# Pooled attention's products taken by turns over the array's column groups, and the last 64 tokens' products and transposes on whole 128-row blocks

## The chip, the cores and the metric

The kernel runs on one core of one Trainium2 chip. The metric is device time in microseconds, the median of repeated executions. The kernel before takes 795.58 us (median of 3, 794.69 to 795.67). TensorE (PE) multiplies, VectorE (DVE), ScalarE (ACT) and GpSimd (POOL) do the elementwise work, SyncE (SP) and ACT issue DMAs.

## The reference

Three stages follow each other: attention (a pooled one plus a local one), a token and channel mixer, and a mixer with sine and cosine.

```python
B, H, S, D = 4, 8, 576, 64; factor = 4; scale = 1 / sqrt(D)
# pooled attention: means over 4 tokens, 144 queries and keys a head
q_d, k_d, v_d = (t.reshape(B, H, S // 4, 4, D).mean(axis=3) for t in (q, k, v))
out_up = repeat(softmax(scale * q_d @ k_d.T) @ v_d, 4, axis=2)
# local attention: |i - j| < 4
out_local = softmax(where(mask, scale * q @ k.T, -1e9)) @ v
x = (out_up + out_local).transpose(0, 2, 1, 3).reshape(B, S, H * D)
# mixer 1: over tokens (576 -> 256 -> 576), then over channels (512 -> 1536 -> 512)
h = relu(x.transpose(0, 2, 1) @ w_tok1) @ w_tok2
u = x + h.transpose(0, 2, 1)
x = u + relu(u @ w_ch1) @ w_ch2
# mixer 2
theta = x @ w_theta
y = w_tok_r @ (x * cos(theta)) + w_tok_i @ (x * sin(theta))
u = x + y
out = u + relu(u @ w_ch)
```

All mixer weights arrive as 64-bit floats.

## The kernel before

The weights are read as pairs of 32-bit words and turned into a high and a low 32-bit part (`weights`, L109 to L153: two ACT passes, a clamp on POOL or DVE, four passes on DVE, one copy on ACT, a subtraction on POOL, a sum on DVE or POOL). Each mixer product is the sum of three (`mm3`, L100): high by high, high by low, low by high. The attention products are plain 32-bit ones; the trace records each of those as two passes, so that 32 products have 64 records.

There are three stretches. First comes the attention stage, up to the end of `ORDER`: for every batch and half of the heads it runs a pooled attention (`quad_front`, events F), four local ones (`pair_local`, L) and the token mixer (`token_mix`, T), mixed with the weight conversions and with channel mixing of the first half of the channels for batches 0 and 1 (C0, C1). The list `ORDER` (L28) says in which order the pieces are emitted; a list scheduler then places each engine's instructions by priority and its own estimate of time, so that an edit in one place moves instructions on every engine. Second, the attention stage's memory is released, and the second half of the channel weights and the weights of mixer 2 are loaded through ACT's DMA queue (`rawq`, L114, L635) and converted beside channel mixing. Third is mixer 2.

In `quad_front` the scores `sd` (L338) and their exponents `pd` are transposed on PE (`pdt`, L383) into `pts`. The second product `od` (L393 to L400) has 144 query rows: its outputs stand in four groups `c` of 32 PSUM partitions, which are the array's four groups of 32 columns. For each group in turn: one product with 260 moving columns (L393), four with 65 (L396), one with 65 in a region of its own (L399), one more added there (L400). All have 128 rows of stationary data and 32 columns. `sd` (L338, L347), the local scores `s` (L448) and the local products `o` (L485) have 64 rows or fewer by 32 columns, and walk over row and column groups by turns.

The tokens 512 to 575 are half a block of 128. In `token_mix` block 4 of the input has the tokens in its first 64 rows; rows 64 to 127 hold copies for the product `xs` (L539), which joins two 64-row products with the low parts. L538 multiplies 64 rows alone; L564 transposes 64 rows to 64 columns. In `pair_local` L476 transposes the ninth slot of `pbuf` (128 rows by 64 columns).

Of the kernel before, what the change touches and what calls it, by code (L numbers as in the profile page):

```python
# [11 lines left out]
F32 = mybir.dt.float32  # L12
# [27 lines left out]
DTOK = 256  # L40
DCH = 1536
NB = 5

NS = 9

STEP, HEADROOM = 102, 2
W = 38
# [4 lines left out]
HEAD = [0, 2, 1, 3]  # L52
# [9 lines left out]
def kernel(  # L62
# [20 lines left out]
    act, dve, pool, pe = nc.scalar, nc.vector, nc.gpsimd, nc.tensor  # L83
# [7 lines left out]
    idt = const.tile([128, 128], F32, name="idt")  # L91
# [144 lines left out]
    with ExitStack() as actx:  # L236
        sb1 = actx.enter_context(tc.tile_pool(name="a1", bufs=1))
# [19 lines left out]
        zero = sb1.tile([128, 384], BF16, name="zero")  # L257
# [6 lines left out]

        msk = sb1.tile([128, NB, W], F32, name="msk")

        pbuf = [sb1.tile([128, NS, 64], F32, name=f"pbuf{i}") for i in range(2)]
        for t in pbuf:
            pool.memset(t, 0.0)

        w1h = sb1.tile([128, 5, DTOK], F32R, name="w1h")
# [6 lines left out]
        def load_tok1():  # L278
            for kb in range(4):
                weights(stg, w1h[:, kb, :], w1l[:, kb, :], [(0, 128, w_tok1[kb * 128 : (kb + 1) * 128, :])])  # L280
            last = w_tok1[512:576, :]
            weights(stg, w1h[:, 4, :], w1l[:, 4, :], [(0, 64, last), (64, 128, last)])
            act.copy(w1s[0:64, :], w1h[0:64, 4, :].bitcast(F32))
            act.copy(w1s[64:128, :], w1l[64:128, 4, :].bitcast(F32))

        def load_tok2():
            for kb in range(2):
# [18 lines left out]
        def quad_front(b, hh):  # L306
# [6 lines left out]
            for p in range(2):  # L313
                p4 = 2 * hh + p
                q, k = loaded[b, p4]
                for src, dst in ((q, qd), (k[:, 3 : 3 + S], kd)):
                    src = src.rearrange("p (s r) -> p s r", r=4)
                    h = sb1.tile([128, SD, 2], F32, tag="qa", name=f"qa_{at}", bufs=1)
# [69 lines left out]
            act.copy(pts[:, 4:7].rearrange("p a n -> p (a n)"), pt[:, 1, 0:384])  # L388
            yield
            od = mmp.tile([128, 512], F32, tag="mm", name=f"od_{at}")  # L390
            for c in range(4):
                r = slice(32 * c, 32 * c + 32)
                pe.matmul(od[r, 0:260], pts[:, 5, r], vl.rearrange("p h d -> p (h d)"), start=True, stop=False)  # L393
                for i in range(4):
                    h = HEAD[i]
                    pe.matmul(  # L396
                        od[r, 65 * h : 65 * h + 65], pts[:, i, r], vs[:, h, :], start=False, stop=(i == 3)
                    )
                pe.matmul(od[r, 260:325], pts[:, 6, r], vl[:, HEAD[c], :], start=True, stop=False)  # L399
                pe.matmul(od[r, 260:325], pts[:, 4, r], vs[:, HEAD[c], :], start=False, stop=True)  # L400
            odv = od[:, 0:325].rearrange("p (h n) -> p h n", h=5)
            rd = sb2.tile([128, 5, 1], F32, tag="rd", name=f"rd_{at}")
# [38 lines left out]
        def pair_local(b, p4):  # L441
            hh, p = divmod(p4, 2)
            at = f"{b}_{p4}"
            q, k = loaded[b, p4]
            s = wide("s", f"s_{at}")
            warm(s[:, 0, 192:512], (12 if b == 0 else 0) + (12 if b == p4 == 0 else 0))
            for i, j, r, g in groups:
                pe.matmul(  # L448
                    s[r : r + 32, j, i // 2 * W : i // 2 * W + W],
                    q[64 * j : 64 * j + 64, 32 * g : 32 * g + 32],  # L450
                    k[64 * j : 64 * j + 64, 32 * g : 32 * g + W],
                    start=True,
                    stop=True,
                )
            pb = pbuf[p4 % 2]
            pv = pb[:, :, 0:W]
            dve.tensor_tensor(
                out=pv[:, 0:8].rearrange("p (b j) n -> p j b n", j=2),
                in0=s[:, :, 0 : 4 * W].rearrange("p j (b n) -> p j b n", n=W),
                in1=msk[:, 0:4].unsqueeze(1).to_broadcast([128, 2, 4, W]),  # L460
                op=ALU.add,
            )
            for j in range(2):
                r = slice(64 * j, 64 * j + 64)
                dve.tensor_tensor(out=pv[r, 8], in0=s[r, j, 4 * W : 5 * W], in1=msk[r, 4], op=ALU.add)
            mx = sb2.tile([128, NS, 1], F32, tag="mx", name=f"mx_{at}")
            dve.tensor_reduce(out=mx, in_=pv, axis=AX.X, op=ALU.max)
            dve.tensor_tensor(out=pv, in0=pv, in1=mx.to_broadcast([128, NS, W]), op=ALU.subtract)
            exps[b, p4] = act.activation(pv, pv, AF.Exp, scale=1.0 / math.sqrt(D))
            yield  # L470
            pt = wide("big", f"pt_{at}")
            pts = sb2.tile([128, NB, 128], F32, tag="plt", name=f"plt_{at}")
            warm(pt[:, 1, 128:512], 12 if b == 0 else 0)
            for blk in range(4):
                pe.transpose(pt[:, 0, blk * 128 : (blk + 1) * 128], pb[:, 2 * blk : 2 * blk + 2, :].rearrange("p j n -> p (j n)"), idt)
            pe.transpose(pt[0:64, 1, 0:128], pb[:, 8, :], idt)  # L476
            act.copy(pts[:, 0:4].rearrange("p b n -> p (b n)"), pt[:, 0, :])
            act.copy(pts[0:64, 4], pt[0:64, 1, 0:128])
            yield
            vw = values[b, p4]  # L480
            o = blocks(wide("o", f"o_{at}"), 65)
            for i, j, r, g in groups:

                h = 0 if i == 8 else 64 * j
                pe.matmul(  # L485
                    o[r : r + 32, 4 if i == 8 else 5 * j + i // 2],
                    pts[h : h + W, i // 2, r : r + 32],
                    vw[h : h + W, g + 2 * j if i == 8 else g, :],
                    start=True,
                    stop=True,  # L490
                )
            rl = sb2.tile([128, 2 * NB, 1], F32, tag="rl", name=f"rl_{at}")
            dve.tensor_scalar(out=rl[:, 0:NS], in0=o[:, 0:NS, 64:65], scalar1=1e-9, scalar2=None, op0=ALU.add)
            dve.reciprocal(out=rl[:, 0:NS], in_=rl[:, 0:NS])
            x = x_of(b, hh)
            dve.tensor_tensor(  # L496
                out=x[:, p, 0:4].rearrange("p b (j n) -> p j b n", j=2),
                in0=o.rearrange("p (j b) n -> p j b n", j=2)[:, :, 0:4, 0:64],
                in1=rl.rearrange("p (j b) n -> p j b n", j=2)[:, :, 0:4].to_broadcast([128, 2, 4, 64]),
                op=ALU.mult,  # L500
            )
            dve.tensor_tensor(
                out=x[:, p, 4, 0:64], in0=o[:, 4, 0:64], in1=rl[:, 4].to_broadcast([128, 64]), op=ALU.mult
            )
            yield
            xu, xe = xus[b, hh]
            xv = x[:, p, 0:4]
            uv = xu[:, 0:4, p * 128 : (p + 1) * 128]
            pool.tensor_tensor(out=xv, in0=xv, in1=uv, op=ALU.add)  # L509
            xv = x[:, p, 4, 0:64]  # L510
            pool.tensor_tensor(out=xv, in0=xv, in1=xe[:, p * 64 : (p + 1) * 64], op=ALU.add)
            halves[b, hh] = halves.get((b, hh), 0) + 1
            if halves[b, hh] == 2:

                first, second = x[:, :, 4, 0:64], x[:, :, 4, 64:128]
                act.copy(second[0:64], first[64:128])
                act.copy(second[64:128], first[64:128])
                act.copy(first[64:128], first[0:64])
            yield

        def token_mix(b, hh):
# [11 lines left out]
            for tb in range(2):  # L533
                ps = mmp.tile([128, 512], F32, tag="mm", name=f"t1_{at}_{tb}")
                t = slice(tb * 128, (tb + 1) * 128)
                for kb in range(4):
                    mm3(ps[:, 0:DTOK], w1h[:, kb, t], w1l[:, kb, t], xh[:, :, kb], xl[:, :, kb], kb == 0, False)
                pe.matmul(ps[:, 0:DTOK], w1h[0:64, 4, t], xh[0:64, :, 4], start=False, stop=False)  # L538
                pe.matmul(ps[:, 0:DTOK], w1s[:, t], xs, start=False, stop=True)  # L539
                h1 = sb2.tile([128, DTOK], F32R, tag="h1", name=f"h1_{at}_{tb}")  # L540
                h2 = sb2.tile([128, DTOK], F32R, tag="h2", name=f"h2_{at}_{tb}")
                act.activation(h1, ps[:, 0:DTOK], AF.Relu)
                dve.scalar_tensor_tensor(
                    out=h2, in0=ps[:, 0:DTOK], scalar=0.0, in1=h1.bitcast(F32), op0=ALU.max, op1=ALU.subtract
                )
                hs.append((h1, h2))
                yield
# [4 lines left out]
            for db in range(2):  # L552
# [3 lines left out]
                for th, (t0, t1) in enumerate(((0, cut), (cut, S))):  # L556
# [2 lines left out]
                    xt = mmp.tile([128, 512], F32, tag="mm", name=f"xt_{at}_{db}_{th}")  # L559
                    first = t0 // 128  # L560
                    for blk in range(first, (t1 + 127) // 128):
                        m = 128 if blk < 4 else 64
                        o = (blk - first) * 128
                        pe.transpose(xt[:, o : o + m], x[0:m, db, blk], idt[0:m, 0:m])  # L564
                    o = t0 - first * 128
                    act.copy(u, xt[:, o : o + n])
                    ps = mmp.tile([128, 512], F32, tag="mm", name=f"t2_{at}_{db}_{th}")
# [296 lines left out]
```

## Time and profile before

| | us |
|---|---|
| median of 3 runs | 795.58 (794.69 to 795.67) |
| the profiled execution | 796.43, its span 794.6 |
| PE busy | 748.0 (94%) |
| DVE busy | 508.9 (64%) |
| ACT, POOL busy | 334.6, 269.5 |
| chain of waits, shares | PE 60%, DVE 21%, DMA 7%, issue 5%, POOL 3% |

The span is cut into 40 equal slices of 19.9 us here; each digit is an engine's busy share in tenths. The last row is the granted TensorE clock in tenths.

```
PE   7788897899999999999889889999999999999998
DVE  5999988863555333379999999722395266455432
PEclk9888998799999999999999999999999999999999
```

PE is busy nearly all the time outside slices 0 to 7 and 19 to 24, and in those two regions DVE is. The share of busy time alone does not say what an engine waits for; the stretches are read apart in the rows below.

### The profile page before, as it was taken

To read this page: it belongs to the slowest core of one execution; us is meant where nothing else is said; L and a number is where in the kernel's file an instruction comes from. 1 tells how busy PE (TensorE), PEld (TensorE's weight loads), DVE (VectorE), ACT (ScalarE), POOL (GpSimd) and SP (SyncE) were. 2 spreads that over 40 slices of the span, in tenths; PEclk is the share of its full clock that TensorE was granted. 3 is DMA by queue.
4 is the path that set the end of the run, shared out by engine and by line. 5 is a ranking of instruction groups with operands and counts; after the bars stand their busy time and mean duration, and the time that the engine had idled before them with its cause. 6 is when DMAs were issued, how large, how long until landed. Compare 5 with 4: busy or idle time off the path is not lost.

```text
span 794.6 us, 19303 instructions
## 1 busy us (share of the span) xinstructions
PE 748.0 (94%) x7872; PEld 697.6 (88%) x7872; DVE 508.9 (64%) x1151; ACT 334.6 (42%) x773; POOL 269.5 (34%) x292
## 2 busy tenths in 40 slices
PE   7788897999999999999889889999999999999998
PEld 4566676888988999999889889999999999999998
DVE  5999988863555333379999999722395266455432
ACT  2555745533334223155556555421285064253210
POOL 1667677732021010078879889300000000000000
PEclk9888998799999999999999999999999999999999
DMA  9578366355423202144646764531000210300101
GB/s 285 161 233 235 115 191 183 93 149 154 154 85 93 85 30 91 60 150 153 193 156 192 239 205 144 162 111 61 31 2 1 90 38 1 120 1 1 61 1 60
DMA packets 61897, 90.73 MB, mean 114 GB/s; under 512 B 10096, under 2 KB 39920, under 8 KB 61808
## 3 DMA queue, kind: packets, MB, share of 16 engines
q1 hardware_dynamic: 53456, 73.70, 30.4%
q10 hardware_dynamic: 8352, 15.80, 6.3%
q8 instruction: 62, 1.02, 0.5%
q14 instruction: 27, 0.22, 0.1%
HBM read 69.42 MB, written 20.05 MB: 113 GB/s over the span
## 4 chain that ended last, share of the span: by engine, by line
PE 60%; DVE 21%; DMA 7%; issue 5%; POOL 3%; ACT 2%; SPq 2%; DVEq 0%; ACTq 0%; POOLq 0%
PE y L103 5%; PE y L101 5%; PE y L102 5%; DVE ww L137 4%; PE c L226 4%; PE c L229 4%; PE c L227 4%; PE c L101 3%; PE c L102 3%; PE c L103 3%; DVE ww L129 2%; DVE we L140 2%; DVE wf L147 2%; POOL ww L125 2%; PE th L101 2%
## 5 line engine op out<-in xcount | busy, mean ns | idle before, releaser
L125 POOL TENSOR_SCALAR ww<-ww 128x256 f32<-128x256 f32 (+1 forms) x85 | 101.2, 1197 | 51.7 <-ACT ww L124 49.9
L103 PE MATMUL y<-wrh,zl 128*128 128x288 f32 x256 | 75.7, 296 | 0.0
L102 PE MATMUL y<-wrl,zh 128*128 128x288 f32 x256 | 75.6, 295 | 0.0
L101 PE MATMUL y<-wrh,zh 128*128 128x288 f32 x256 | 75.6, 296 | 0.0
L218 DVE SCALAR_TENSOR_TENSOR g<-c,g 128x288 fp32r<-128x288 f32 x96 | 43.2, 452 | 48.0 <-ACT g L217 47.6
L226 PE MATMUL c<-g,c21h 128*128 128x288 f32 x192 | 54.4, 305 | 11.1 <-ACT g L217 11.0
L217 ACT ACTIVATE g<-c 128x288 fp32r<-128x288 f32 x96 | 38.7, 408 | 58.1 <-PE c L103 58.0
L101 PE MATMUL c<-uh,c10h 128*128 128x288 f32 x192 | 58.4, 309 | 0.7 <-DVE g L218 0.7
L103 PE MATMUL c<-uh,c10l 128*128 128x288 f32 x192 | 57.8, 302 | 0.0
L102 PE MATMUL c<-ul,c10h 128*128 128x288 f32 x192 | 57.1, 298 | 0.0
L226 PE MATMUL c<-g,c20h 128*128 128x288 f32 x192 | 54.6, 309 | 2.5 <-ACT g L217 2.0
L101 PE MATMUL c<-uh,c11h 128*128 128x288 f32 x192 | 56.9, 296 | 0.0
L122 ACT ACTIVATE wf<-raw 128x256 bf16<-128x256 uint32 (+1 forms) x91 | 40.3, 443 | 39.2 <-DVE wrl L150 6.0
L102 PE MATMUL c<-ul,c11h 128*128 128x288 f32 x192 | 56.7, 295 | 0.0
L509 POOL TENSOR_TENSOR x<-x,xu 128x512 f32<-128x512 f32 x16 | 23.1, 1454 | 98.7 <-DVE x L496 51.8
L103 PE MATMUL c<-uh,c11l 128*128 128x288 f32 x192 | 56.5, 294 | 0.0
L227 PE MATMUL c<-g,c21l 128*128 128x288 f32 x192 | 53.4, 301 | 0.0
L227 PE MATMUL c<-g,c20l 128*128 128x288 f32 x192 | 53.4, 300 | 0.0
L129 DVE TENSOR_SCALAR ww<-ww 128x256 uint32<-128x256 uint32 (+1 forms) x91 | 46.3, 510 | 5.2 <-POOL ww L125 5.0
L231 DVE TENSOR_TENSOR ut<-c,ut 128x288 f32<-128x288 f32 x56 | 25.3, 451 | 36.7 <-PE c L229 36.5
L226 PEld LDWEIGHTS c<-g,c21h 128*128 128x128 f32 x192 | 36.9, 192 | 13.5 <-ACT g L217 13.5
L137 DVE SCALAR_TENSOR_TENSOR ww<-raw,ww 128x256 uint32<-128x256 uint32 (+1 forms) x91 | 47.8, 528 | 1.1
(202 smaller groups left out, 2394.1 us busy)
## 6 DMA issues: line engine op xcount, KB each, us to landing
raw<-w_ch ACTq DMA_DIRECT2D x32, 256.0 KB, 2.9
ut<-uT SPq DMA_DIRECT2D x14, 576.0 KB, 4.3
xT<-ut SPq DMA_DIRECT2D x14, 576.0 KB, 3.1
raw<-w_ch SPq DMA_DIRECT2D x24, 256.0 KB, 3.4
vd<-vtok SPq DMA_DIRECT2D x8, 650.0 KB, 6.0
raw<-w_ri ACTq DMA_DIRECT2D x18, 288.0 KB, 3.0
k<-kT SPq DMA_DIRECT2D x16, 291.0 KB, 5.1
q<-qT SPq DMA_DIRECT2D x16, 288.0 KB, 3.8
```

What stands on the lines that cost most here:

```text
L101: pe.matmul(out, lh, rh, start=start, stop=False)
L102: pe.matmul(out, lh, rl, start=False, stop=False)
L103: pe.matmul(out, ll, rh, start=False, stop=stop)
L122: act.activation(f, words[:, :, 0], AF.Copy, scale=2.0**-52)
L125: next(clamps).tensor_scalar(out=w, in0=w, scalar1=F64_LEAST, scalar2=F64_MOST, op0=ALU.max, op1=ALU.min)
L129: dve.tensor_scalar(out=wu, in0=wu, scalar1=3, scalar2=0x3FFFFFF8, op0=ALU.logical_shift_left, op1=ALU.bitwise_and,)
L137: dve.scalar_tensor_tensor(out=wu, in0=words[:, :, 1], scalar=0xC0000000, in1=wu, op0=ALU.bitwise_and, op1=ALU.bitwise_or)
L217: act.activation(h1, ps[:, 0:HALF], AF.Relu)
L218: dve.scalar_tensor_tensor(out=h2, in0=ps[:, 0:HALF], scalar=0.0, in1=h1.bitcast(F32), op0=ALU.max, op1=ALU.subtract)
L226: pe.matmul(ps[:, 0:HALF], w2h[:, cb, d], hs[cb][0], start=(cb == 0), stop=False)
L227: pe.matmul(ps[:, 0:HALF], w2l[:, cb, d], hs[cb][0], start=False, stop=False)
L229: pe.matmul(ps[:, 0:HALF], w2h[:, cb, d], hs[cb][1], start=False, stop=(cb == NCB - 1))
```

## The change

The `od` products are emitted by rounds: the four 260-column products, one for each column group, then the four groups' products for each head, then the four L399s, then the four L400s. The products themselves and their number stay. The ninth slot of `pbuf` gets a tenth, always zero, beside it, so that its transpose is a 128 by 128 one. L538 takes all 128 rows: rows 64 to 127 of the weight block are set to zero once by a copy on ACT, after the two copies that need them. The transposes of block 4 in `token_mix` take all 128 rows and columns.

```diff
-        pbuf = [sb1.tile([128, NS, 64], F32, name=f"pbuf{i}") for i in range(2)]
+        pbuf = [sb1.tile([128, NS + 1, 64], F32, name=f"pbuf{i}") for i in range(2)]
...
             act.copy(w1s[64:128, :], w1l[64:128, 4, :].bitcast(F32))
+
+            act.copy(w1h[64:128, 4, :], zero[64:128, 0:DTOK])
...
-            for c in range(4):
-                r = slice(32 * c, 32 * c + 32)
+
+            rows = [slice(32 * c, 32 * c + 32) for c in range(4)]
+            for r in rows:
                 pe.matmul(od[r, 0:260], pts[:, 5, r], vl.rearrange("p h d -> p (h d)"), start=True, stop=False)
-                for i in range(4):
-                    h = HEAD[i]
-                    pe.matmul(
-                        od[r, 65 * h : 65 * h + 65], pts[:, i, r], vs[:, h, :], start=False, stop=(i == 3)
-                    )
+            for i in range(4):
+                h = HEAD[i]
+                for r in rows:
+                    pe.matmul(od[r, 65 * h : 65 * h + 65], pts[:, i, r], vs[:, h, :], start=False, stop=(i == 3))
+            for c, r in enumerate(rows):
                 pe.matmul(od[r, 260:325], pts[:, 6, r], vl[:, HEAD[c], :], start=True, stop=False)
+            for c, r in enumerate(rows):
                 pe.matmul(od[r, 260:325], pts[:, 4, r], vs[:, HEAD[c], :], start=False, stop=True)
...
-            pv = pb[:, :, 0:W]
+            pv = pb[:, 0:NS, 0:W]
...
-            for blk in range(4):
-                pe.transpose(pt[:, 0, blk * 128 : (blk + 1) * 128], pb[:, 2 * blk : 2 * blk + 2, :].rearrange("p j n -> p (j n)"), idt)
-            pe.transpose(pt[0:64, 1, 0:128], pb[:, 8, :], idt)
+            for blk in range(NB):
+                src = pb[:, 2 * blk : 2 * blk + 2, :].rearrange("p j n -> p (j n)")
+                pe.transpose(pt[:, blk // 4, blk % 4 * 128 : blk % 4 * 128 + 128], src, idt)
...
-                pe.matmul(ps[:, 0:DTOK], w1h[0:64, 4, t], xh[0:64, :, 4], start=False, stop=False)
+                pe.matmul(ps[:, 0:DTOK], w1h[:, 4, t], xh[:, :, 4], start=False, stop=False)
...
-                        m = 128 if blk < 4 else 64
                         o = (blk - first) * 128
-                        pe.transpose(xt[:, o : o + m], x[0:m, db, blk], idt[0:m, 0:m])
+                        pe.transpose(xt[:, o : o + 128], x[:, db, blk], idt)
```

PE, the `od` of batch 1's second half of the heads, before (`c` is channel mixing; the pattern of four rows stands four times):

```order
L101 MATMUL c_0_0_1_3_3217<-uh_0_1_3156,c10h 128x288
L393 MATMUL od_1_2861<-vl_1_2571,pts_1_2805 32x260
L396 MATMUL od_1_2861<-vs_1_2569,pts_1_2805 32x65 x4
L399 MATMUL od_1_2861<-vl_1_2571,pts_1_2805 32x65
L400 MATMUL od_1_2861<-vs_1_2569,pts_1_2805 32x65
L393 MATMUL od_1_2861<-vl_1_2571,pts_1_2805 32x260
...
```

The same place in the changed kernel (L396, L400, L402 and L404 are its new line numbers):

```order
L489 MATMUL o_1_2910<-vw_1_2534,plt_1_2854 32x65 x14
L396 MATMUL od_1_2862<-vl_1_2572,pts_1_2806 32x260 x4
L400 MATMUL od_1_2862<-vs_1_2570,pts_1_2806 32x65 x16
L402 MATMUL od_1_2862<-vl_1_2572,pts_1_2806 32x65 x4
L404 MATMUL od_1_2862<-vs_1_2570,pts_1_2806 32x65 x4
L489 MATMUL o_1_2910<-vw_1_2534,plt_1_2854 32x65 x13
```

The group's products now follow each other by kind, and it stands between local products `o` where it stood within channel mixing.

PE, the last transposes of the token mixer (`xt`, batch 3), before:

```order
L229 MATMUL c_2_0_0_3_5111<-g_2_0_0_5_5048,c20h 128x288
L564 MATMUL xt_1_1_1_4911<-idt,x_1_4692 128x128 x2
L564 MATMUL xt_1_1_1_4911<-idt,x_1_4692 128x64
L101 MATMUL c_2_0_1_0_5228<-uh_0_1_5224,c10h 128x288
L102 MATMUL c_2_0_1_0_5228<-ul_0_1_5225,c10h 128x288
```

The same in the changed kernel:

```order
L226 MATMUL c_2_0_0_3_5112<-g_2_0_0_2_4997,c20h 128x288
L567 MATMUL xt_1_1_1_4912<-idt,x_1_4693 128x128 x3
L227 MATMUL c_2_0_0_3_5112<-g_2_0_0_2_4997,c20l 128x288
L226 MATMUL c_2_0_0_3_5112<-g_2_0_0_3_5014,c20h 128x288
```

The 64-column transpose is a third whole one, and the group moved forward past the end of a channel product: 727 channel products stand ahead of the attention stage's last instruction on PE before, 715 now.

ACT, the end of the attention stage, where it issues the first load of the second weights (`raw`), before (`us` is the token mixer's result, `g` a channel product's):

```order
L566 COPY us_1_1_4898<-xt_1_1_1_4911 128x320
L217 ACTIVATE g_2_0_1_0_5241<-c_2_0_1_0_5228 128x288
L217 ACTIVATE g_2_0_1_1_5258<-c_2_0_1_1_5245 128x288
L114 DMA raw<-w_ch 128x256 x2
L217 ACTIVATE g_2_0_1_2_5275<-c_2_0_1_2_5262 128x288
```

The same in the changed kernel:

```order
L569 COPY us_1_1_4899<-xt_1_1_1_4912 128x320
L217 ACTIVATE g_2_0_1_0_5242<-c_2_0_1_0_5229 128x288
L114 DMA raw<-w_ch 128x256 x3
L217 ACTIVATE g_2_0_1_1_5259<-c_2_0_1_1_5246 128x288
```

The loads stand one channel block earlier in ACT's queue.

## Rows read from the trace of the kernel before

**Rows 1.** Busy time by stretch: us, then each engine, granted clock, DMA share, GB/s.

```profile
20.00:160.00 140.00, 119.15 (x1999) 95.31 (x1997) 128.05 (x324) 78.79 (x215) 99.97 (x111) 0.85 0.59 174
160.00:337.00 177.00, 175.13 (x2326) 159.15 (x2325) 79.60 (x198) 55.02 (x130) 24.19 (x29) 1.00 0.33 99
337.00:505.00 168.00, 153.11 (x1106) 148.62 (x1105) 153.71 (x342) 91.26 (x227) 140.88 (x144) 0.99 0.58 181
```

**Rows 2.** Timeline of ACT where the attention stage ends: start, length, instruction.

```profile
336.17 0.41 ACT L217 ACTIVATE g<-c 128x288 fp32r<-128x288 f32 x1 [1.17 <-PE c L103]
336.72 0.91 ACTq L114 DMA_DIRECT2D raw<-w_ch  x2
337.75 0.41 ACT L217 ACTIVATE g<-c 128x288 fp32r<-128x288 f32 x1 [1.17 <-PE c L103]
```

**Rows 3.** Timeline of PE over one `od` group, the eighth.

```profile
257.76 0.62 PE L393 MATMUL od<-vl,pts 128*32 128x260 f32 x2
258.22 0.62 PE L396 MATMUL od<-vs,pts 128*32 128x65 f32 x8
258.68 0.22 PE L399 MATMUL od<-vl,pts 128*32 128x65 f32 x1
258.68 0.41 PE L393 MATMUL od<-vl,pts 128*32 128x260 f32 x1
...
258.79 0.28 PE L400 MATMUL od<-vs,pts 128*32 128x65 f32 x2
...
261.56 0.28 PE L400 MATMUL od<-vs,pts 128*32 128x65 f32 x2
261.77 0.26 PE L448 MATMUL s<-k,q 64*32 64x38 f32 x4
```

**Rows 4.** Timeline of PE's weight loads in the same group.

```profile
258.68 0.14 PEld L393 LDWEIGHTS od<-vl,pts 128*32 128x32 f32 x2
```

**Rows 5.** Groups of PE's instructions up to 330 us, forms apart.

```profile
L393 PE MATMUL od<-vl,pts 128*32 128x260 f32 x64 | 20.5, 402 | 0.0
...
L538 PE MATMUL t<-xh,w1h 64*128 64x256 f32 x16 | 6.9, 431 | 0.0
...
L564 PE MATMUL xt<-idt,x 64*128 64x64 f32 x15 | 4.1, 273 | 0.0
```

**Rows 6.** Timeline of PE, one group of local products.

```profile
120.13 1.09 PE L485 MATMUL o<-vw,plt 38*32 38x65 f32 x72
```

**Rows 7.** Timeline of PE without the 64-row product L538 (87 us), and with it.

```profile
87.28 0.28 PE L102 MATMUL t<-xl,w1h 128*128 128x256 f32 x1
...
87.63 0.28 PE L101 MATMUL t<-xh,w1h 128*128 128x256 f32 x1
...
241.41 0.28 PE L102 MATMUL t<-xl,w1h 128*128 128x256 f32 x1
...
242.28 0.28 PE L102 MATMUL t<-xl,w1h 128*128 128x256 f32 x1
```

**Rows 8.** Timeline of PE: three transposes, the last of 64 rows (294 us); whole ones.

```profile
294.24 0.58 PE L564 MATMUL xt<-idt,x 128*128 128x128 f32 x3
...
295.00 0.31 PE L102 MATMUL t<-w2l,h 128*128 128x320 f32 x1
...
300.51 0.38 PE L475 MATMUL pt<-idt,pbuf 128*128 128x128 f32 x2
...
300.83 0.38 PE L564 MATMUL xt<-idt,x 128*128 128x128 f32 x2
...
301.19 0.29 PE L102 MATMUL c<-ul,c10h 128*128 128x288 f32 x1
```

**Rows 9.** The chain of waits, 84 to 112 us: start, length, what.

```profile
105.31 1.01 PE od L393 x2
```

**Rows 10.** Timeline of PE at a wait.

```profile
127.41 1.09 PE L475 MATMUL pt<-idt,pbuf 128*128 128x128 f32 x4 [3.24 <-DVE x L502]
```

**Rows 11.** Busy time after that wait, columns as in rows 1.

```profile
128.00:132.00 4.00, 3.59 (x16) 3.21 (x15) 3.86 (x13) 2.70 (x9) 2.81 (x5) 0.50 1.02 222
```

## The prediction

> **What bounds the kernel now.** I read the busy time by stretch first, because the share over the whole span (PE 94%) mixes stretches with different limits. From 160 to 337 us PE is busy 175.13 of 177.00 us at the full granted clock, DVE only 79.60: here a microsecond of PE is a microsecond of the kernel. From 20 to 160 us DVE is busy 128.05 of 140 us and PE 119.15 at a mean clock of 0.85: here the weight conversions bind, and PE counts only where the chain runs through it. From 337 to 505 us DVE is at 153.71 and POOL at 140.88 of 168 us, and PE has 15 us idle [rows 1]. After 505 us PE is full again, as the last slices of the page show; the change touches nothing there.
>
> The second view is ACT's queue at the border. The loads that feed the bound of 337 to 505 us are issued at 336.72, after the attention stage has let go of its memory [rows 2]. So that stretch hangs on the end of the attention stage and moves forward with it as a block; what PE saves ahead of it is not eaten by PE's idle time in it.
>
> The third view is PE's timeline of one `od` group. Its first pass starts at 257.76 and the next product after it at 261.77: 4.01 us. A 260-column product (two passes) holds its column group for 0.46 us, from 257.76 to 258.22; four 65-column products (eight passes) for another 0.46, so 0.057 a pass. Only at the border of two column groups do two of them work at once: at 258.68 the next group's 260-column pass starts in the same moment as this group's first L399, and this group's L400 still follows at 258.79, two passes of 0.055 later, as fast as without a neighbour [rows 3]. So column groups do run side by side, and the order of the program is what keeps three of the four idle. The weight load of that neighbour also starts at 258.68, under the running product [rows 4].
>
> **The change part by part.** *The `od` rounds.* Each column group has 0.46 + 12 x 0.057 = 1.15 us of work (two long passes, eight of L396, four of L399 and L400). If the four groups run beside each other, that is the time of the whole `od`. What lies behind its last pass stays: that pass starts 0.06 after 261.56, and the next product 0.15 later, at 261.77, so about 0.1 more than a pass. The new step is 1.26 us; saved 2.75 a group. That more than two tiles run at once is shown by the local products, which go round eight tiles: 72 passes in 1.09 us, 0.22 of it the last one's length, so 0.012 a pass against 0.057 here [rows 6]. The bounds: at best the 64 passes at 0.012, which the 1.15 us of one group's own work forbids; at worst no gain, 4.01. I take 1.26, next to the rows of the local products. There are eight groups (64 records of L393, eight each [rows 5]); four of them start after 160 us, the one of rows 3 last: 4 x 2.75 = 11.0 us.
>
> The weighing of a rule. The row shows a load into one column group while another column group's product runs, both on all 128 rows [rows 4]. The Trainium skill says otherwise: in "TensorE: Matmul & The Clock Gate", Part 3, a weight load overlaps a running product only when their row groups differ. All `od` products use the same four row groups, so by that rule each load would wait for the product ahead and the rounds would gain nothing. The trace speaks against it at this place, and the rule stands below as a rival.
>
> *The 64-row product (L538).* With it, four steps from one L102 to the next take 242.28 - 241.41 = 0.87 us; three plain steps take 87.63 - 87.28 = 0.35, so four 0.47 [rows 7]. The excess is 0.40 us, and it is not the product itself (256 columns either way) but the two changes between 64-row and 128-row tiling, each with a wait on both sides. Of the 16 [rows 5] ten lie after 160 us: 4.0 us.
>
> *The 64-row transposes (L564).* Three transposes and the first product behind them take 295.00 - 294.24 = 0.76 us. With whole ones it is 301.19 - 300.83 = 0.36 for two and the product, and 0.107 more for a third ((300.83 - 300.51) / 3): 0.47 [rows 8]. Saved 0.29. Of the 16 (one is past the row's 330 us) eleven lie in the PE-bound stretch; six stand before 128-row work and save 0.29, five before 64-row products, where one of the two changes stays, and I give these 0.1, a third. Together 2.2 us.
>
> *The transposes of the ninth slot (L476)* take 0.10 us, 300.73 to 300.83, as long as the whole one beside them: nothing. *The zero copy* on ACT is one more of the two 64 by 256 copies there, 0.40 us in a queue that is busy 78.79 of 140 us [rows 1]; DVE's conversions cover it, and uncovered it costs 0.4 once. *The larger memset* of `pbuf` is 11% of 0.58 us, twice, before the first load lands: nothing, at most 0.13.
>
> *What the scheduler moved.* On PE the changes between 64-row and 128-row forms, counted in the order from the fifth `od` on, go from 94 to 69. The edits alone take away 32 (two for each of ten L538s and six L564s), so seven came back, at about 0.17 each: 1.2 us lost. ACT issues the second weights' loads one channel block earlier, and a block is 337.75 - 336.17 = 1.58 us [rows 2]: 1.6 gained. The work jumped over lands in the next stretch, where PE has 15 us to spare.
>
> *Before 160 us* there are four `od` groups, six L538s and five L564s, some 15 us of PE. DVE's 91% bounds what can come of it: between 0 and 10. Only one of the groups is on the chain, at 105.31, with its first product at half speed in either order (1.01 instead of 0.46 us) [rows 9]: 2.75 saved there as well. With 0.4 for each of three L538s I take 4; behind it DVE's queue is late next.
>
> *The sum.* 11.0 + 4.0 + 2.2 - 1.2 + 1.6 + 4 = 21.6 us. From the profiled execution's own 796.43 that leaves 774.8; the median of the runs shown is 0.85 below it, so I predict 774.
>
> **The rivals.** *One pass at a time per group.* The first pass of each product runs beside the others' work, but its second pass holds up the issue behind it. Then a group costs one pass of every product: 16 x 0.057 + 8 x 0.057 + 4 x 0.23 = 2.3 us, 2.4 with the tail, and the saving falls to 1.6: 4.6 us less in the bound stretch, about 1 less before it, 780. For it: inside one column group passes are strictly serial [rows 3]. Against it: 0.012 a pass in the local products, each of which is a pair too [rows 6].
>
> *No overlap: the change doesn't do what it says.* The `od` stays at 4.01; left are 4.0 + 2.2 - 1.2 + 1.6 and 1 before 160 us: 788. Against it: rows 3 and 4. This is what the skill's rule on row groups gives.
>
> *The end of the attention stage is set by something other than PE.* A faster PE then waits for DVE, POOL or the trip of `od` through memory. In the bound stretch PE idles only 1.9 us [rows 1], so nothing shows yet, but little shows how far behind the next chain is. If half of the 17 us there is lost: 783 to 785.
>
> *More comes before 160 us.* All of DVE's idle time goes, 10 instead of 4: 768.
>
> *Slower: the clock.* At 127.41 PE had waited 3.24 us for DVE, and the granted clock in the next four microseconds was 0.50 [rows 10, 11], that is 1.2 GHz instead of 2.4. The two slices of 19.9 us from there on have 8 and 7 tenths of the clock on the page, so up to 0.5 x 19.9 = 10 us were lost to it. PE now reaches DVE's results sooner, so such waits can appear between 160 and 337 us, where there is none now. Each costs up to 3 + 10 us; two use up the gain, and from there on the kernel is slower: 796 to 800.
>
> **How the numbers follow.** Forecast 0.60 (own range 769 to 780), one pass at a time 0.13, no overlap 0.06, another end 0.08, more before 160 us 0.06, the clock 0.07. The range for 8 in 10 is 765 to 787, from the case with more to the edge of no overlap. A measurement of this kernel can tell about 0.2%, 1.6 us. Only the clock reaches that on the other side; I split it 0.04 slower and 0.03 the same. Faster is 0.93.
>
> **What would show it.** In the new trace the first passes of the four long `od` products start within a few hundredths of a microsecond and a whole `od` lasts about 1.2 us; 2.4 is the first rival, 3.9 the second. The 64-row product's steps become 0.12 us. The first `raw` load of ACT is issued between 312 and 318 us, and from there to the end of the conversions it is again some 168 us. The prediction fails if PE has idle time or a clock below 1.00 in the stretch before that load, or if the conversions afterwards take longer than before.

## The result, and the profile after

The changed kernel takes 771.94 us (median of 4, 770.8 to 773.74) against 795.13 for the kernel before beside it: a ratio of 0.9714, 95% interval 0.9688 to 0.9741. The forecast was 774 with a range of 765 to 787. A second measurement on another chip gave 773.15 against 795.8, 0.9721 (0.9702 to 0.974). The profiled execution has a span of 768.9 us, 25.7 less than before, and lies at the lower end of the four. In the table of the experiments one execution of 2314.4 us (C1 last, again) was in a slower state and is left out of its median.

First the same view as [rows 1], cut where the parts of the program end: at the first load of the second weights, at the end of their conversion, at the end. Before the change (us, PE, weight loads, DVE, ACT, POOL, granted clock, DMA share, GB/s):

```profile
0.00:336.72 336.72, 308.71 (x4566) 263.30 (x4567) 217.75 (x548) 138.72 (x354) 127.73 (x147) 0.93 0.47 141
336.72:507.10 170.38, 155.49 (x1124) 151.00 (x1123) 155.72 (x347) 91.66 (x228) 141.73 (x145) 0.99 0.58 181
507.10:794.60 287.50, 283.77 (x2186) 283.33 (x2185) 135.40 (x258) 104.19 (x191) 0.00 (x0) 1.00 0.13 43
```

And after:

```profile
0.00:314.18 314.18, 273.35 (x4554) 236.53 (x4555) 219.99 (x547) 136.86 (x354) 126.18 (x147) 0.94 0.51 150
314.18:480.00 165.82, 156.15 (x1125) 151.35 (x1124) 153.78 (x347) 92.37 (x229) 139.24 (x145) 0.99 0.60 185
480.00:768.90 288.90, 285.14 (x2197) 284.71 (x2195) 135.82 (x259) 104.33 (x191) 0.00 (x0) 1.00 0.14 44
```

Ahead of the first load PE has 35.4 us less to do, and 12.8 us of that became idle time (28.0 before, 40.8 now); 22.5 us are gained there. The conversions are 4.6 us shorter and what follows 1.4 longer: 3.2 more. The counts of PE differ by 12, the channel products that moved across the border.

The `od` group that answers to [rows 3], timeline of PE:

```profile
239.73 0.65 PE L396 MATMUL od<-vl,pts 128*32 128x260 f32 x8
240.19 0.64 PE L400 MATMUL od<-vs,pts 128*32 128x65 f32 x32
240.65 0.29 PE L402 MATMUL od<-vl,pts 128*32 128x65 f32 x8
240.76 0.30 PE L404 MATMUL od<-vs,pts 128*32 128x65 f32 x8
240.99 0.37 PE L452 MATMUL s<-k,q 64*32 64x38 f32 x32
```

From 239.73 to 240.99 are 1.26 us, where it was 4.01. Eight long passes take 0.46, as two did; 32 short ones take 0.46, as eight did: four column groups at once, each at the pace that it has alone. The weight loads of the eight long passes, from PE's timeline of loads, start together with them, while the passes take until 240.19:

```profile
239.73 0.16 PEld L396 LDWEIGHTS od<-vl,pts 128*32 128x32 f32 x8
```

The place of [rows 7]: L542 is the product that had 64 rows.

```profile
225.36 0.28 PE L102 MATMUL t<-xl,w1h 128*128 128x256 f32 x1
225.48 0.28 PE L103 MATMUL t<-xh,w1l 128*128 128x256 f32 x1
225.60 0.28 PE L542 MATMUL t<-xh,w1h 128*128 128x256 f32 x1
225.72 0.29 PE L102 MATMUL t<-xl,w1h 128*128 128x256 f32 x1
```

It has become one step of 0.12 among others. Its weight load starts at 225.48, in the moment in which the product L103 ahead of it starts on the same 128 rows and 128 columns:

```profile
225.48 0.19 PEld L542 LDWEIGHTS t<-xh,w1h 128*128 128x128 f32 x1
```

The transposes, answering to [rows 8]:

```profile
298.94 0.49 PE L567 MATMUL xt<-idt,x 128*128 128x128 f32 x3
299.19 0.38 PE L226 MATMUL c<-g,c20h 128*128 128x288 f32 x1
299.40 0.30 PE L227 MATMUL c<-g,c20l 128*128 128x288 f32 x1
```

Three transposes and the product behind them take 0.46 us, 0.76 before. ACT's queue at the border, answering to [rows 2]:

```profile
313.63 0.41 ACT L217 ACTIVATE g<-c 128x288 fp32r<-128x288 f32 x1 [3.78 <-PE c L103]
314.18 1.38 ACTq L114 DMA_DIRECT2D raw<-w_ch  x3
```

The first load is issued at 314.18, inside the 312 to 318 that the prediction named, behind one channel block's `g` instead of two.

### The profile page after: what moved, and what is told of

The parts are those of the page before. It is cut to its first block, busy times and chain, and to the rows that moved or that the text cites. A ratio compares the mean times of both kernels' runs of the same rounds, so it can differ in the third digit from the quotient of the medians.

```text
span 768.9 us, 19289 instructions
## 1 busy us (share of the span) xinstructions
PE 714.6 (93%) x7872; PEld 672.6 (87%) x7872; DVE 509.6 (66%) x1151; ACT 333.6 (43%) x774; POOL 265.4 (35%) x292
## 4 chain that ended last, share of the span: by engine, by line
PE 60%; DVE 23%; DMA 6%; issue 6%; POOL 2%; SPq 2%; ACT 1%; ACTq 0%; DVEq 0%; POOLq 0%
PE y L103 5%; PE y L101 5%; PE y L102 5%; PE c L229 4%; PE c L226 4%; PE c L227 4%; DVE ww L137 4%; DVE ww L129 3%; PE c L101 3%; PE c L103 3%; PE c L102 3%; DVE wf L147 3%; DVE we L140 3%; PE th L101 2%; PE th L102 2%
## 5 line engine op out<-in xcount | busy, mean ns | idle before, releaser
L103 PE MATMUL y<-wrh,zl 128*128 128x288 f32 x256 | 75.7, 296 | 0.0
L102 PE MATMUL y<-wrl,zh 128*128 128x288 f32 x256 | 75.6, 295 | 0.0
L122 ACT ACTIVATE wf<-raw 128x256 bf16<-128x256 uint32 (+1 forms) x91 | 40.4, 444 | 45.5 <-DVE wrl L150 8.3
L102 PE MATMUL c<-ul,c10h 128*128 128x288 f32 x192 | 57.2, 299 | 1.0 <-DVE ul L98 1.0
L103 PE MATMUL c<-uh,c10l 128*128 128x288 f32 x192 | 57.5, 300 | 0.0
L102 PE MATMUL c<-ul,c11h 128*128 128x288 f32 x192 | 56.6, 295 | 0.0
L103 PE MATMUL c<-uh,c11l 128*128 128x288 f32 x192 | 56.5, 294 | 0.0
L129 DVE TENSOR_SCALAR ww<-ww 128x256 uint32<-128x256 uint32 (+1 forms) x91 | 50.0, 551 | 6.3 <-POOL ww L125 5.8
L226 PE MATMUL c<-g,c20h 128*128 128x288 f32 x192 | 53.0, 302 | 0.7 <-ACT g L217 0.5
L102 PEld LDWEIGHTS y<-wrl,zh 128*128 128x128 f32 x256 | 48.1, 188 | 0.0
L101 PEld LDWEIGHTS y<-wrh,zh 128*128 128x128 f32 x256 | 48.1, 188 | 0.0
L103 PEld LDWEIGHTS y<-wrh,zl 128*128 128x128 f32 x256 | 48.1, 188 | 0.0
```

The lines of the kernel that those rows point to most:

```text
L101: pe.matmul(out, lh, rh, start=start, stop=False)
L102: pe.matmul(out, lh, rl, start=False, stop=False)
L103: pe.matmul(out, ll, rh, start=False, stop=stop)
L122: act.activation(f, words[:, :, 0], AF.Copy, scale=2.0**-52)
L129: dve.tensor_scalar(out=wu, in0=wu, scalar1=3, scalar2=0x3FFFFFF8, op0=ALU.logical_shift_left, op1=ALU.bitwise_and,)
L226: pe.matmul(ps[:, 0:HALF], w2h[:, cb, d], hs[cb][0], start=(cb == 0), stop=False)
```

## The experiments

The table has for each kernel the median beside the kernel before on the same chip, and from its profile: the first load, PE's busy and idle time ahead of it, the granted clock there, and the time from the load to the end. All are sums of the windows shown or of windows cut alike.

| kernel | us (before) | ratio, 95% | first load | PE busy, idle | clock | rest |
|---|---|---|---|---|---|---|
| before | 795.13 | | 336.7 | 308.7, 28.0 | 0.93 | 457.9 |
| changed | 771.94 (795.13) | 0.9714, 0.9688 to 0.9741 | 314.2 | 273.4, 40.8 | 0.94 | 454.7 |
| changed, again | 773.15 (795.80) | 0.9721, 0.9702 to 0.9740 | 317.8 | 278.4, 39.3 | 0.91 | 453.6 |
| `od` rounds alone | 783.60 (795.59) | 0.9856, 0.9836 to 0.9877 | 324.9 | 291.8, 33.1 | 0.92 | 457.3 |
| rows alone | 787.97 (795.59) | 0.9907, 0.9888 to 0.9926 | 332.6 | 297.7, 34.9 | 0.94 | 455.2 |
| `od` by pairs | 780.11 (795.59) | 0.9816, 0.9794 to 0.9838 | 323.1 | 287.5, 35.6 | 0.93 | 457.4 |
| tenth slot alone | 794.57 (795.59) | 0.9992, 0.9978 to 1.0006 | 334.5 | 305.5, 28.9 | 0.94 | 458.0 |
| 128-row product alone | 793.94 (795.80) | 0.9981, 0.9966 to 0.9995 | 333.7 | 303.4, 30.3 | 0.94 | 458.3 |
| whole transposes alone | 791.42 (795.80) | 0.9937, 0.9916 to 0.9958 | 333.6 | 299.6, 34.0 | 0.95 | 456.5 |
| loads one block later | 774.25 (796.28) | 0.9728, 0.9700 to 0.9756 | 315.3 | 277.4, 37.8 | 0.93 | 456.4 |
| C1 last | 770.57 (796.28) | 0.9677, 0.9647 to 0.9706 | 289.8 | 250.8, 39.0 | 0.93 | 480.0 |
| C1 last, again | 772.38 (795.80) | 0.9712, 0.9687 to 0.9736 | 290.7 | 250.3, 40.4 | 0.94 | 479.9 |
| C1 before the last token mixer | 776.26 (796.28) | 0.9739, 0.9705 to 0.9773 | 299.7 | 261.1, 38.6 | 0.93 | 475.4 |
| clamps on POOL | 774.73 (796.28) | 0.9735, 0.9702 to 0.9768 | 313.1 | 275.4, 37.6 | 0.93 | 457.7 |

**The `od` rounds alone.** Edit, against the kernel before:

```diff
-            for c in range(4):
-                r = slice(32 * c, 32 * c + 32)
...
+            for i in range(4):
+                h = HEAD[i]
+                for r in rows:
+                    pe.matmul(od[r, 65 * h : 65 * h + 65], pts[:, i, r], vs[:, h, :], start=False, stop=(i == 3))
...
```

> The kernel before with the rounds of od alone; the 64-row product and the 64-row transposes stay. Theory (PE time): each of the eight od groups falls from 4.01 to 1.26 us between its first pass and the next product, 22 us of PE less ahead of the first load of the second weights. The full change took 35.4 us of PE busy time off that stretch and made it 22.5 us shorter, a worth of 0.64; so 14 us gained, 781 us. Rival (a lucky order of the scheduler): the groups also take 1.26 us, but the time follows the new order of the other engines and lies 4 us or more away from 781 on either side.

Measured 12.0 us gained, 14 expected. The eighth group takes 1.25 us here too, as PE's timeline of this kernel shows (start, duration, step, count):

```profile
244.56 0.65 PE L394 MATMUL od<-vl,pts 128*32 128x260 f32 x8
245.02 0.64 PE L398 MATMUL od<-vs,pts 128*32 128x65 f32 x32
245.47 0.30 PE L400 MATMUL od<-vl,pts 128*32 128x65 f32 x8
245.59 0.30 PE L402 MATMUL od<-vs,pts 128*32 128x65 f32 x8
245.81 0.59 PE L450 MATMUL s<-k,q 64*32 64x38 f32 x43
```

From 244.56 to 245.81 all four column groups are at work at once. PE's busy time ahead of the load fell by 16.9 us, not 22; the granted clock there was 0.92. The time lies 2.6 us from the forecast, inside the 4 that were to tell the rival.

**The rows alone.** Edit, against the changed kernel: the `od` loop of before.

```diff
-            rows = [slice(32 * c, 32 * c + 32) for c in range(4)]
-            for r in rows:
+            for c in range(4):
+                r = slice(32 * c, 32 * c + 32)
...
```

> The changed kernel with od column group by column group again: whole 128-row products, transposes and the tenth slot alone. Theory (PE time): od stays at 4.01 us; 16 products save 0.40 each and 16 transposes 0.1 to 0.29, together about 9.5 us of PE, worth 0.64: 6 us gained, 789 us. With the od rounds alone it adds up to the whole gain of 23 us within 3. Rival (a lucky order): the two parts do not add up; this one lies outside 786 to 792.

Measured 7.6 us gained, within the range. Added to the rounds alone that is 19.6 of the 23.2 and 22.7 us of the whole: 3.6 and 3.1 are missing, just past the 3 that were allowed; the intervals of the three ratios are some 1.5 to 2.1 us each, so that this is at the edge of the noise. The table shows where: the load comes 11.8 us earlier with the rounds alone and 4.1 with the rows, 16.0 together, and 22.5 and 19.0 earlier with both. Behind the load the parts add up (0.6 and 2.7 us, 3.2 and 4.3 with both). Whether the parts help each other ahead of the load or the profiled executions differ by their clock (0.92 with the rounds alone) is not shown.

**The `od` by pairs of column groups.** Edit, against the changed kernel:

```diff
-            rows = [slice(32 * c, 32 * c + 32) for c in range(4)]
-            for r in rows:
-                pe.matmul(od[r, 0:260], ...
+            for pair in (0, 2):
+                rows = [(c, slice(32 * c, 32 * c + 32)) for c in (pair, pair + 1)]
+                for c, r in rows:
+                    pe.matmul(od[r, 0:260], ...
...
```

> The changed kernel with od by turns over two column groups at a time, 0 and 1, then 2 and 3. Theory (column groups run side by side, each with 1.15 us of its own work): a group from first pass to next product takes 2 x 1.15 + 0.1 = 2.4 us, less up to 0.2 where the second pair's long pass starts beside the first pair's last ones; 8 x 1.0 us of PE more than in the changed kernel, at a worth of 0.64 some 5 to 6 us: 777 us. Rival (what counts is only that neighbours in the order differ): about 1.3 us a group and no change against 772. Rival (the order of the scheduler): the time lies outside 774 to 780.

Timeline of PE for its eighth group:

```profile
246.65 0.63 PE L397 MATMUL od<-vl,pts 128*32 128x260 f32 x4
247.11 0.62 PE L401 MATMUL od<-vs,pts 128*32 128x65 f32 x16
247.57 0.22 PE L403 MATMUL od<-vl,pts 128*32 128x65 f32 x2
247.58 0.41 PE L397 MATMUL od<-vl,pts 128*32 128x260 f32 x2
...
248.61 0.28 PE L405 MATMUL od<-vs,pts 128*32 128x65 f32 x4
248.82 0.36 PE L453 MATMUL s<-k,q 64*32 64x38 f32 x31
```

2.17 us from 246.65 to 248.82. In the time of two long passes there are now four, and the second pair starts beside the first pair's last products, as single groups did before. 1.26, 2.17 and 4.01 us for four, two and one group at a time: what each group has of its own work stays, and the number at once divides it, but for what overlapped at the borders already. That settles the mechanism and rules out the rival in which it is enough that neighbours differ. The time, 780.1, is 3 us over the forecast and 0.1 us past the bound that I had set for the order. 7.4 us of PE (8 x 0.92) went with 7 to 8 us of time, but by the table 2.7 to 3.8 us of the difference lie behind the load, where the pairs have the 12 channel products in the place of before (457.4 from the load to the end against 454.7 and 453.6). Ahead of it the load comes 8.9 or 5.3 us later, 1.6 of it for these products, so that the worth of PE's time lies between 0.5 and 1 here; 0.64 is neither shown nor refuted.

**The tenth slot and the zero copy alone.**

```diff
-        pbuf = [sb1.tile([128, NS, 64], F32, name=f"pbuf{i}") for i in range(2)]
+        pbuf = [sb1.tile([128, NS + 1, 64], F32, name=f"pbuf{i}") for i in range(2)]
...
+            act.copy(w1h[64:128, 4, :], zero[64:128, 0:DTOK])
...
```

> The kernel before with the parts of the change that should cost and gain nothing: the tenth zero slot with whole transposes of it, and the zero copy into the weight block; od, the 64-row product and the 64-row transposes stay. It shows how far an edit without any work of its own moves the time through the scheduler's order. Theory (PE time): 795 us, within 2. Rival (order): 3 us or more from 795 on either side.

No change that can be measured, as expected: the 1.0 us lies within the interval. This one edit without work of its own moves the time through the scheduler by less than the noise. PE's busy time ahead of the load is 3.2 us lower even so (305.5 against 308.7, at a clock of 0.94 instead of 0.93): differences of that size between two profiles are no sign of saved work.

**The 128-row product alone, and the whole transposes alone.**

```diff
-                pe.matmul(ps[:, 0:DTOK], w1h[0:64, 4, t], xh[0:64, :, 4], start=False, stop=False)
+                pe.matmul(ps[:, 0:DTOK], w1h[:, 4, t], xh[:, :, 4], start=False, stop=False)
```

> The kernel before with the whole 128-row product in place of L538 alone (and the zero copy that it needs). Theory (PE time): 16 x 0.40 = 6.4 us of PE, ahead of the first load; at a worth between 0.64 and 1, 4 to 6 us gained: 789 to 791 us. Rival (the gain of the rows comes from the transposes or from the order): 793 or more.

```diff
-                        pe.transpose(xt[:, o : o + m], x[0:m, db, blk], idt[0:m, 0:m])
+                        pe.transpose(xt[:, o : o + 128], x[:, db, blk], idt)
```

> The kernel before with whole 128-row transposes in place of the 64-row ones alone. Theory (PE time): 7 or so of 16 save 0.29 and the others 0.1, 3 us of PE, 2 to 3 us gained: 792 to 793 us. Rival (order): outside 790 to 795.

Measured 1.9 and 4.4 us, the other way round than expected. The first, 793.94, is 2 us short of the 4 to 6 and on the rival's side (793 or more); the second, 791.42, is 0.6 us under its 792, within the bounds that shut out the order. With the slot's 1.0 they make 7.3 of the 7.6 that the rows give together. The piece itself is saved in the first as well: four steps from one L102 to the next with the product among them take 0.47 us, where they took 0.87 [rows 7].

```profile
240.65 0.28 PE L102 MATMUL t<-xl,w1h 128*128 128x256 f32 x1
...
241.12 0.28 PE L102 MATMUL t<-xl,w1h 128*128 128x256 f32 x1
```

So 16 pieces of 0.40 us brought 1.9 us alone; why not more is not shown. PE's busy time ahead of the load fell by 5.3 and 9.1 us, of which some 3 can be chance, as the slot shows. The second has the 12 channel products moved behind the load (x4554 below), 1.6 us of PE, and a clock of 0.95; how the rest divides I can't tell. The busy time up to the first load of the product alone (columns as in the first view of the result):

```profile
0.00:333.68 333.68, 303.42 (x4566) 260.17 (x4567) 219.15 (x548) 138.89 (x355) 128.76 (x147) 0.94 0.47 143
```

And of the whole transposes alone:

```profile
0.00:333.58 333.58, 299.63 (x4554) 255.98 (x4555) 217.71 (x547) 136.87 (x353) 127.79 (x147) 0.95 0.47 141
```

Against [rows 1] cut at 336.72 with its 308.71 us of PE, the counts are those of before in the first (x4566) and 12 fewer in the second.

**The first loads one block later.** Edit, against the changed kernel: the first six conversion steps are emitted behind the second `g` of the next half of the tokens, and issued after it.

```diff
+        late = half == 0 and b == 2
...
-                    act.activation(h1, ps[:, 0:HALF], AF.Relu)
+                    relu = act.activation(h1, ps[:, 0:HALF], AF.Relu)
...
+                if late and th and cb == 1:
+                    with tc.issue_after(relu.ins):
+                        for st in islice(aside, per):
+                            st()
...
-            for st in islice(aside, per):
+            for st in islice(aside, 0 if late and not th else per):
```

> The changed kernel, in which the first loads of the second weights stand one channel block later in ACT's queue, where they stood in the kernel before; nothing else is meant to move. In the changed kernel and in the one with the rows alone those loads stand one block earlier than in all others here, and in these two alone the time from the first load to the end is 454.7 to 455.2 us, 457.3 to 458.0 in the others. Theory (the place of the loads sets both): first load 1.6 us later, and the rest longer by 3, so 776 to 777 us. Rival (something else in the new order shortens the stretch): 773 to 774 us, the 1.6 alone or nothing.

The 776 to 777 of the theory did not come: 774.25, a ratio of 0.9728 where the changed kernel has 0.9714 and 0.9721, though the interval (to 0.9756) reaches up to it. Beside the first profile of the changed kernel the load is 1.1 us later, the conversions are 1.6 longer, and what is behind them is the same, as its busy time by stretch from the load on shows (columns as before):

```profile
315.28:482.72 167.44, 154.36 (x1116) 151.13 (x1115) 155.68 (x346) 92.33 (x229) 137.37 (x145) 0.98 0.59 181
482.72:771.60 288.88, 285.16 (x2197) 284.72 (x2195) 135.85 (x259) 104.15 (x191) 0.00 (x0) 1.00 0.14 44
```

DVE's busy time in the conversions is back at 155.7, as in the kernel before, where the changed kernel has 153.8 and 153.2 in its two profiles. DVE's idle time there is 11.8, as in the changed kernel (12.0 and 11.4), and not 14.7 as before. So some 2 us of DVE's work go with the place of the loads; that DVE waits some 3 us less has another cause, which stays open.

**Channel mixing of batch 1 last.** Edit, against the changed kernel: in the order's list, `C1` goes from ahead of the token mixers 6 and 7 to the end.

```diff
-T5 T5 V14 L14 F7 L13 L13 T5 T5 L13 F7 T5 T5 F7 T5 T5 V15 L15 C1 T6 T6 L14 L14 T6 L14 T6 T6 L15 L15 T6 L15 T6
+T5 T5 V14 L14 F7 L13 L13 T5 T5 L13 F7 T5 T5 F7 T5 T5 V15 L15 T6 T6 L14 L14 T6 L14 T6 T6 L15 L15 T6 L15 T6
...
```

> The changed kernel with channel mixing of batch 1 at the end of the list of the order, so that 540 channel products stand ahead of the attention stage's last instruction on PE, 715 in the changed kernel. Theory (from the first load on, DVE's conversions set the time and PE's idle 10 us there are free): the first load comes 175 x 0.133 = 23 us earlier less what PE then idles for want of filler, say 10 to 15 us earlier; PE's idle time of 9.7 us in the conversions takes up part of the products pushed back and the rest lengthens what lies behind. Net gain 4 to 8 us: 764 to 768 us. Rival (PE needs those products as filler between the attention stage's waits): no gain or a loss, 772 or more.

> The changed kernel with channel mixing of batch 1 at the end of the order's list, a second time, beside the changed kernel. In its first run the first load came 24.4 us earlier, the conversions took 14.4 us longer and what lies behind them 10.8 us longer. Theory (the products that moved bring their DVE steps into the stretch that DVE binds, so that nearly all is given back): 0 to 2 us under the changed kernel, not to be told apart from it. Rival (PE's idle time in the conversions was free): 3 us or more under it.

The first measurement, 770.57, lies between the 764 to 768 of its theory and the 772 of the rival; the second, 772.38, came as its theory said. The load came 24.4 us earlier, more than I expected, and nearly all of it was given back, as the three stretches of this kernel show (first of the two runs, columns as before):

```profile
0.00:289.78 289.78, 250.75 (x4379) 214.33 (x4380) 215.55 (x534) 133.91 (x346) 126.36 (x147) 0.93 0.54 158
289.78:469.98 180.20, 169.22 (x1247) 165.78 (x1246) 157.18 (x355) 92.71 (x234) 136.07 (x145) 1.00 0.56 170
469.98:769.70 299.72, 293.94 (x2250) 293.27 (x2248) 139.03 (x265) 105.76 (x194) 0.00 (x0) 0.99 0.15 48
```

The 22.6 us of PE taken from the front stand again behind: 13.1 in the conversions, which became 14.4 longer, and 8.8 behind them. DVE's share has fallen to 157 of 180 us while PE's is 94%, as in the changed kernel. My theory, that the products bring DVE steps along, explains 3.4 us of DVE, not 14.4. What the rows show is that PE's 10 us of idle time there are no room for more products: 9.7 us are idle before the move and 11.0 after it. Beside the changed kernel on one chip, 772.38 against 773.15 (ratios 0.9712 and 0.9721), the two can't be told apart.

**C1 ahead of the last token mixer.** Edit, against the changed kernel: `C1` stands two steps ahead of the run of `T7`.

```diff
-... V15 L15 C1 T6 T6 L14 L14 T6 L14 T6 T6 L15 L15 T6 L15 T6 T6 T6 T7 T7 ...
+... V15 L15 T6 T6 L14 L14 T6 L14 T6 T6 L15 L15 T6 L15 T6 C1 T6 T6 T7 T7 ...
```

> As the one with channel mixing of batch 1 last in the list, but ahead of the last token mixer's pieces: 597 channel products ahead of the attention stage's last instruction. Theory (DVE's conversions bind from the first load on): about two thirds of the other one's shift, 766 to 770 us. Rival (filler): no gain, 772 or more.

The load came 14.5 us earlier, the rest became 20.7 longer; 776.26, the rival's side, and not 766 to 770. This is no gain either.

**All clamps on POOL.**

```diff
-    clamps = chain(islice(cycle([pool] * 4 + [dve]), 33), repeat(pool))
+    clamps = repeat(pool)
```

> The changed kernel with all clamps of the first weights on POOL; before, every fifth of the first 33 was on DVE. Theory (DVE binds up to about 150 us, 136.8 of 152 us busy, and PE has 35 us idle there): 6 clamps of about 0.4 us leave DVE, 2 us gained at most, 770 us. Rival (POOL's clamp takes 1.2 us and stands ahead of DVE's own steps for the same block): no gain or 1 to 3 us lost.

774.73 at a ratio of 0.9735, not to be told from the changed kernel. Up to 152 us POOL clamps 31 blocks instead of 24, 36.5 us instead of 28.3. The load comes 1.1 us earlier than in the changed kernel's first profile and the rest is 3.0 longer, with the 12 channel products ahead of the load as before. None of these versions beats the changed kernel by more than the noise.

**The changed kernel once more**, with no edit.

> The changed kernel once more, as it is, beside the others of this round on one chip: 0.971 of the kernel before, some 772 to 773 us. It is there to be compared with the next one.

Its three stretches, cut as in the first view:

```profile
0.00:317.76 317.76, 278.42 (x4554) 242.28 (x4555) 218.41 (x547) 137.43 (x354) 127.11 (x147) 0.91 0.50 148
317.76:482.43 164.67, 155.23 (x1125) 151.32 (x1124) 153.23 (x347) 92.35 (x229) 139.71 (x145) 0.99 0.60 187
482.43:771.30 288.87, 285.15 (x2197) 284.72 (x2195) 135.85 (x259) 104.18 (x191) 0.00 (x0) 1.00 0.14 44
```

The same program with the same counts needs 5.1 us more of PE ahead of the load, at a clock of 0.91 instead of 0.94, and issues it 3.6 us later. So some of the 22.5 us of the first profile is that execution's clock.

## Why the prediction was right

The size of each saved piece of PE's work was right to a hundredth of a microsecond: an `od` group 1.26 forecast and 1.26 measured, a step of 0.12 for the 64-row product, three transposes 0.47 and 0.46. The reason for the largest was right as well, since pairs give 2.17. The rule that weight loads overlap only across row groups ("TensorE: Matmul & The Clock Gate" of the Trainium skill, Part 3) does not hold here: the eight loads at 239.73 run under products on the same 128 rows, and by that rule alone nothing would have been saved. Nor is this special to column groups, since the load at 225.48 runs under a product that has its rows and its columns; so the load in [rows 4] was no sign of column groups side by side, and the products' own times are.

The sum of 21.6 us against 22.7 to 23.2 came out partly by luck: errors on both sides met. The step that was most mis-sized is *before 160 us*, put at 4. PE's timeline at the start of the third and the fifth `od` group, before the change:

```profile
105.24 1.08 PE L393 MATMUL od<-vl,pts 128*32 128x260 f32 x2
...
164.70 0.62 PE L393 MATMUL od<-vl,pts 128*32 128x260 f32 x2
```

And after:

```profile
100.53 0.65 PE L396 MATMUL od<-vl,pts 128*32 128x260 f32 x8
...
152.20 0.65 PE L396 MATMUL od<-vl,pts 128*32 128x260 f32 x8
```

The third, with the same products and seven transposes more ahead of it, starts 4.7 us earlier. The fifth starts 12.5 us earlier, with 16 channel products and 25 local ones fewer ahead of it (2.1 and 0.6 us by their steps): 9.8 us gained, and 8.7 in the second profile, where it starts at 153.34. That is the 10 of the rival *more comes before 160 us*, if not its 768. DVE's 91% did not hold the gain down to 4; along which waits it came is not followed here.

In the stretch that I called PE-bound the forecast was 16.0 (11.0 + 4.0 + 2.2 - 1.2), and 22.5 - 9.8 - 1.6 = 11.1 came, 8.7 in the second profile. PE idles there 6.2 us (162.18 less 156.02, from 152 us to the load) where it was 1.9 (from 160 us): the sign that I named for a failure did show, at a quarter of the gain. More than half of it lies before 172 us, where DVE is busy 17.53 of 20 us in the first profile and 19.55 in the second (columns as in the first view):

```profile
152.00:172.00 20.00, 16.67 (x298) 14.63 (x298) 17.53 (x45) 7.48 (x21) 14.85 (x18) 1.00 0.54 158
152.00:172.00 20.00, 15.29 (x285) 13.13 (x285) 19.55 (x46) 7.50 (x20) 15.57 (x18) 0.99 0.47 146
```

PE's longest waits there end with DVE's steps `ods` (1.3 us, 1.9 in the second) and `us` (0.8, 1.4). So DVE is the chain that was closer behind than "1.9 us of idle" told, and the rival in which something other than PE sets the end came in part.

The conversions were to take some 168 us again and took 165.8 and 164.7 (170.4 before, in the same cut), the rest 1.4 more: 3.2 and 4.3 us that no step had. They come with the 12 channel products behind the load, in all four profiles that have them there (453.6 to 456.5 from the load on, 457.3 to 458.3 in those that have them ahead of it; 456.4 with the loads alone put back, and more where `C1` was moved). The part of them that is DVE's work goes with the place of the loads; the cause of the rest is not shown. The 1.6 us that I counted for the earlier load was no gain in itself: behind the conversions PE has 2197 products instead of 2186, and that is where the 1.4 us come back. The premise that PE has room to spare in the conversions was wrong, as C1 last shows too.

Of the rivals, one pass at a time and no overlap are excluded by the timelines. The clock rival is seen at work, but small: as a spread of some microseconds between executions of one program, and with one wait of the kind that it named: in the second profile PE is busy 2.20 of the four microseconds from 168, and the next four are at a granted clock of 0.62, in a stretch that had 1.00 before.

```profile
172.00:176.00 4.00, 4.00 (x22) 4.00 (x22) 0.89 (x3) 1.01 (x3) 0.00 (x0) 0.62 0.44 149
```

The sixth group starts at 178.43 there and at 174.48 in the first profile, 1.1 us of which the fifth has already: between the two groups 2.8 us were lost beside the first profile, and not up to 13.

## What to carry to other kernels

Products that fill only 32 of the array's columns should be emitted by rounds over the four column groups, with the accumulation within a group kept in order: the products stay the same and took less than a third of the time here (1.26 us instead of 4.01). A single 64-row product among 128-row ones costs two changes of tiling, 0.4 us here; fill it up with zero rows, but expect less in the kernel's time than in PE's (1.9 us for 16 of them alone). And when PE's work is cut on a stretch, expect a part of it back as idle time even where PE looked full, and check by moving work whether idle time in a later stretch is free before counting on it.

## What the hardware showed beside

Four column groups take two-pass 32-bit products at once with no loss to any: 0.46 us for eight passes of 260 columns, as for two. A weight load runs under a product on the same rows and columns (both start at 225.48). And one program's granted clock ahead of the load was 0.94 in one execution and 0.91 in another, 5.1 us of PE apart, with the same instructions.
